# Another replay order and other PSUM banks for the same instructions of a Zipformer block on one core

## The chip, the cores and the metric

The kernel runs on one core of a Trainium2 chip. The time is device time in microseconds (us) of one execution. The core's engines each work through a list of instructions of their own: PE (TensorE, matmuls, with a separate queue PEld for loading weights), ACT (ScalarE, activation functions), DVE (VectorE), POOL (GpSimd) and SP (SyncE, which here only issues DMA transfers). Engines wait for one another through semaphores. Lower is better.

## The reference

`x` has 2 batch elements of 4000 tokens of 144 channels in bf16. There are 4 heads of 36 channels; the feed-forward parts are 576 wide; the convolution has 5 taps.

```python
h = _layernorm(x); h = _silu(h @ w_ff1a) @ w_ff1b; x = x + 0.5 * h
q, k, v = heads(_layernorm(x) @ w_qkv)              # 4 heads of 36
p = _softmax((q @ k^T) * 36 ** -0.5)                # 4000 x 4000 for each head
x = x + heads_back(p @ v) @ w_o
h = _layernorm(x) @ w_pw1; a, b = h[..., :144], h[..., 144:]
h = a * _sigmoid(b)
c = sum over 5 taps of hp[:, i:i + T, :] * dw[i]    # depthwise, padded by 2 on each side
x = x + _silu(c) @ w_pw2
h = _layernorm(x); h = _silu(h @ w_ff2a) @ w_ff2b; x = x + 0.5 * h
return _layernorm(x)
```

## The kernel before

**Tiling.** The 8000 tokens are 16 chunks of 500 (CH), 8 for each batch element; a chunk is 4 blocks of 125 rows (TB), kept in SBUF as X. For a chunk, `pre` does the first feed-forward part and q, k, v; then comes attention; `post1` does the output projection with its residual, the next normalisation and the gated pair (GLU); `post2` the convolution, its residual, the second feed-forward part, the last normalisation and the store. The attention of a chunk is a row of steps, each one key tile of 64 keys and two heads: `emit_S` lets PE compute scores into two PSUM banks, `emit_exp` lets ACT take their exponential (128 x 1000, tile PT), and `emit_O` (`o_quads`) lets PE multiply the result with V. For 190 of the tiles DVE does the exponential instead, in four instructions (`dve_tile`). The work of `pre`, `post1` and `post2` of other chunks is laid between these steps.

**Normalisation.** `ln` takes statistics on DVE (tile ST), variance plus epsilon (RS), a power of -1/2 on POOL, and then the normalised rows (XN). At the start and at the end this is DVE's work but for the power, two blocks at a time; in between POOL does all but the statistics. The rows are then transposed for the matmuls (tile XT): on PE at the start and the end, and otherwise by `blocks`: a 32 x 32 transpose on DVE, a write to DRAM by four transfers ("rows"), and a read back by two, both from SP's queue. SP's queue also holds the loads of X and the stores of the output.

**The order.** All instructions are recorded through one method, `Rec.op` (so that nearly every row of the profile has the same line, L419, the one that issues them), while a planner with costs of its own walks the threads. The recorded instructions form blocks: those that one step of the planner gave to one engine. `Rec.reorder` then replays them in an order that is written out in the table ORDER. It has a string for each engine with one character for each block; the character's place in ALPHABET less 45 is by how many places the block goes later or earlier than in the planner's list (`P` is no shift; `~` starts a larger one):

```python
codes, shift = [ALPHABET.index(c) for c in table[e]], []
...
    shift.append(c - 45)
...
    at[i + shift[i]] = blk
lines[e] = [o for blk in at for o in blk]
```

Semaphore waits are derived afterwards (`Rec.finish`), from what each instruction reads and writes. An engine works strictly in its list's order, so a block that waits holds up all behind it. The table PLACES has a digit for each of the 1724 PSUM tiles, the first bank that it gets (`Rec.place`); a tile waits for those who used its banks before.

**The start.** The load of chunk 0 comes in two halves by SP (`X[0:TB, 0:2, :]` and `X[0:TB, 2:NB, :]`, semaphores of their own). DVE's list starts with memsets (`zero_k`, `early`, `setup_v`) and the statistics of chunk 0's blocks 0, 1 and 2, 3. PE runs filler matmuls on the identity (`warm`) until there is something to do.

Of the kernel before, what the change touches and what calls it, by code (L numbers as in the profile page):

```python
# [13 lines left out]
H = 4  # L14
# [25 lines left out]
        "PPPPPPPPQOPPPPROQNPPQRPQLPPRPTPUPNIZOVOKVVL~OOKOK~OUHINSNLMMMOPNOJSOOL[I[KMYMKOGRNJHFKOOOE^NNN_dMKLM"  # L40
        "nXMJ@LJMFMYGaJNKMJhLLLLljKKKKKKWKMMWNKK`BJJJQRecHFSIGKH]QKMRGKPMJJMMQTNPNXTRSUJUJJJSLPMPPQUQQNKOTOOR"
        "OQLPPPPPYOOPN[NNNOMfRNLYULMIMOS^KIMOJNaNNQMNHPPaUOMQNYKPSPPQUSVV^QQ^_Q5<@QCPMKIMNNTQMSMNSNUOYQKMMOQQ"
        "^MSOORNOPPCOORPZP^O]OOO[OCNOQEHMUJNNTOMR[MQWXMPMMNNDMPXSNNZMMTMMMTMPLMPP]OOOOQQNUKNOMQMP]WNOMPNVKYPN"
        "JNQHNOOPQQQMPPQOPUP]MNNNOOTNNOMNWOPPMPNOW]VNN[MMHMKYMMQ]YKI`JLQYJJKV[KHMJTLJOJPMQORPVMQNYMN]MN[bLLLL"
        "LMNLPRPKWOYFMNOVNOHXXMKOLNNNN[[_MMMTLLTKKKLJOOPRP`MO_OMNOMPQLLMRMMMPPPQOSYP[MOOISOLNPPIPSPTOLRNNWPNO"
        "QQMMPUQRN[QQQRJFPPPPJQQSPPKQQNPPPPVPPQOPVXOOPNDNPRROSVSYNFWMPYUPNDPJFPNPTOPYOLOPNQ[NLNRPMRLNNOPhUNZM"
        "MMNLNNPMMWYLPNZKNLMF[LPPSLVINLNOMWQNYPYPLQHKOSNORPGPPPS[OOLOOPPYLNNNVOMNOM^QMNTOO_KMMNOMPPLPNQOYL]RY"
        "LMKLMMPLY]KLNNQXMRXSLI[MDObNOENPMMNSNNQMMWNNNOSVNiKZNNQOTFNNOMXXUMMMM?TLLIYMQXXLLMMQZMJJ`ORLMUMKQYNL"
        "INPMMUVNLNOMYPMOORNNRUNKPNO_ROQLSSKMQMKPROLPSOORNOSOOOTVNNNNSNTMTMNNOVXNOMORLSNVXIMSYLMKLN^XYNLMNHMM"
        "WLLMXMNYMOLNNXMNXMMVMM[SLJLLZN^OLNNJUbLLLQNLPRGNNOOOPNRNOPPPeOOOOPSOOORROf`OPNO^@QDLJLMOLTKLTMTRKGMQ"  # L50
        "QNUOPNROYYPZOHNbILLLLbTLLSLLLLPLM_M[MMMMMcMMMMNLMOdZMNNNNIMMMMXMNNVOMKMMZNOUaMMMQMM]^HOMKNNNJZMKM[LM"
        "QgLLLMWMMMMU]LLLV^MQJMWTMHBHMZSKL[PLLZTMK_bMMIGbMPLPQMSVCKRKSMBINPPSPVOLOOOOZQNNS[MMMMNSMOMNO]aNNcMM"
        "MMMMMMNLNNNZWNZMZPNKPMYBENOPJYNNPMPQOLQNPPRRO[YQJNOPQOPXFPHPNOOOPWOOOOOOXPMTQOLOK^OXNNOMPPPLPPHQQNgR"
        "cOLQOMPNOOOOdRM@LdOJOIPIOOOJOOOOJOOPNUPNOOQQYLQ]NLZ[LLLdWKIKLLLWULE]LLLLLOMWRcKLLLNZM[PMMRILNKZJ`[JK"
        "MOLLUbKeJLLYKOUKMMMMMY=KMNNZNL^NLNNNNNN_NNNOQQNPTHNN_NLOOO^QMNPKO^QQM_JFPLOPJMNPPLPhMPROOPQOWOWNNNNU"
        "U?NO[HMTOOOCNOOOQO[OQOUOOOPHVORPYMGNPPMOVNN[QOVKPNZPGLOY]OPLOPPPBHOOORPRROR`OPWQNZCLNNPQZKMQETOJOMNU"
        "OOOOOPPPP[OOPNQNQRLMVZLOTNKPLLOOPPVPNOVOMRMOSLOOPPPPPZOWOMNNN]NLMPRTLNZUNLQMNYWNRAOPTOSHRNDQOPTOOPNP"
        "UOUQ_LROQQIQFNOYPNUKQNKTNKOQRSTNQNRXFQOQVQULMVEMPPP[PPPQODZcMPMMQINPKMPNOOOPRMNPPPQOZOOOOOQOMOOPXOOZ"
        "NNNNNN`NPWMXNNOPNKOCNOXPNOQOMZQMUOKXMZP[^XIMMOOKPABPJOPPPXOOQOPPPRIOPSOVSMOTKQUKLPNQNPXQOMROMPMQWQMU"
        "OQNJMQQNPQQTQOKTNO[NQOPQOUOOVRMUZPNVSYMN`OQK6TNNZ;NLNVMMMMTMMVWMMdMNLMNOO]N[MMM]XLJKKRK^aJHNPPRKNX>N"  # L60
        "OJLOMNPPPSPPQTVOOQVPLPQOAPQOPQOQZVOLOMRUMKL[MPMOOQWMMNNYOLNORNNNOYVNNNOWLMMROORROH]QNQMNOXNOMPMUPKMY"
        "NTOLORSTJMWOPPFObTYLNQSMKG_MKMNN`RMKLOLR]MKPNgIMMMNOYNKNNNNNZTMQXILIXJLMQLYOSJMNPU_]JLOKRSMMHLMOMQOW"
        "OOQOMOUNPNUQRM`YYLOREKNKKV[LJNLOSQJN`KPXLObLMWNK]MIJQLLOUO^LDLTKQNLVLQ^MMQRMSFMUWMNNWMG^MTRMJYLRPNGO"
        "TYMN[aXVMWQHKLJMFRf[M5LMNSNNKNLZMNNQRPLJTOIOO`^YMMNLMMOMKMMNRSLROLPPTOVOOLVNNPMOO_ROOLRNNNQQMMRNNPQO"
        "VQNNTVNLMPMZUO_QOLLOSNNVNOQNNQSPSWNWNPNVNN[QMNRPNQVXMNPMXPPXKUNNNNVQM~N?ZRMMMPXRLM]LLSMNLNQOMO[NQORO"
        "TNPPY[K]SBNNKILMNNPNPP_TNNOMN_NNNNNPMMSNNNNQYMPNOVZNNYJLN`]MMRMNRCOPLPNVOQ@USLMMNQOQ[NOOUNNNNNNTNQNN"
        "[QNNOOZRMMPMZPNPGM`N`NLMMR[OPLQNGGLOZWNOOOFPMMOPPPPQOQOQRRRSQJRPYPVPQOPPU@QUXEPMRIQNQJQQUPQUPIPYJNPW"
        "WPKOKVOYHJiMPPLJOPTOOIOPROOIUOMNORLQLQQQMRPQQLTOQRRSUUOHHNRMO"
    ),
    "act": (  # L70
        "PPPPPPPPPPPPPRTNNOOPPQOPPPPPPXPNOSNNNNPPPPQOPPSPNOQZQORKRSLLOQQJPPPPQQNQOPPPPPPPPPQQQMPPQOPPPPPPPPRO"
        "OPQOPQQNPPPPPPPPPPPPPPPPPPPPPPPPPPPPPPPPPPPPPPPPPPPPPPPPPPPPPPPPPPPPPQOPPPROSNOOPPPPPPPPPQOPPPPPPPPP"
        "QOPPPPPPPPPPPQOPPPPPPPPPPPPQOPPPPPPPPPPPRPNPQOPPPPPRPNPPPPPPPPPPPPPPPPPPPPPPPPPPPPPPPPPPPPPPPPPPQOQQ"
        "NPPPPPPPPPPPPPPPPPPPPPPPPPPPPPPPPPPPPPPPPPPPPPPPPPPPPPPPPPPPPPPPPPPPPQOPPPPPPPPPPPPPPQOPPQOPPPPPPPPP"
        "PQOPPPPPPPPPPPPPPPPPPPPPPPPPPPROOPQOPPPPPPPPPPPPPPPPPPPQOPPPPQOPPPPPPPPPPPPPPPPPROOQQQMPPPPPPPPPPPPP"
        "PPPPPQOPPQOPPPPPPPQOPPPPPPPPPPQOPPQOPPPPQQQQQKQQNPPPPPPQOPPPPPPPPPPPPPPPQOPPPQOPPPPPPPPPPPPPPPPPPPPQ"
        "OPPPPPPPTOOOOROOPPPPPPPPPPPPPPPQOPQOPPPPPPPPPPQOPPQOPPPPPPPQOPPPPPPPPPPQOPPPPQOQOPPPPPPPPQOPPPPPPPPP"
        "QOPRPNQOPPPPPPPQOPPPPPPPPPPPPPPPPPPPPPQRNOPPPQOPPPPPPPQQNPPPPPPPPQOPPPPPPPQOQOPPQOPPPPPPPPPPQOPPPPPP"
        "PPPQOQOPPPPPPPPPPPPPPPPPPPPPPPPPQOPQQNPPPPPPPPPPPPPPPPPPPPROOPPPPPPPPPPPQQNPPPPPPPPQOPPPPPPPPPPPPPPP"
        "PPPPPQOPPPPPPPRPNQOPPPPPPPQOPPPPPPPPPPPPQOPPPPPPPPPPPPPPPPPPPPPPPPPPPPPPQOPPPPPPPPPPPPPPQOPPPPPPPPPP"  # L80
        "PPPPPPPPPPPPPPPPPPPPPPPPPPPPPQOPPRORPMSPPULOSNRMMPPPPQTPSOKSQOKROORPQQLPPPPPPRORRRWRJRRMHMROO"
    ),
    "dve": (
        "PUO[VM~P6~P6~P)~P6ILIKKLDKMJQRJJJKIKQKKLJKMKOLJWOILJHLJNQNPHFGNNNJMMMMBMWOIKIMINLMNOODNDPSPLORCFVSWC"
        "JDJSIOMBREEMKNCMMMMFNNJMMMMMMNLOPSPROLPPRPNPQOQOQQQMQOQQNPQQNQOPPQOPPQOPPPQOROOPROQVQOYPNOPROSPXURVQ"
        "UU;JNIQQSSSOSQRSSZRSSSKRVQUJ=OO)PROQNPRPRSLPRPQJQOPPPUOPNPQ`VPVOVOMEULFNKNRMRPQQQQIQOPQOQOSOORNTNOPN"
        "QOPQOPPQOQOPPPRPNPROQRMQRPQRPTPPPRPVVPNPSOLQQQQQQ5PPVPPPPPQRHQQQLPPPPPPPPQOPPPPPPPPPROSNPNPPPQSQSLSO"
        "RJQQLQQQQQQQQHPPROSPPTRPNQGQOPQOUQOPLQNRPNPQORUNNOOQNSOOTRUOMTOOPFPQOPPPPPPQQRRRKMRPNPQOPPPPPPPPPPQR"
        "PRPQQQHQOPWOPSOSKTLVOSNUNQMDOPPROOSOPNSQO^PjOOOSNNNCMNTMPLMNTNNNNNOOOPROOROOPRPQQRPJPRSNNQNPQOQOPQOQ"
        "OYRNNNYNOMNSOLRMULQNNOTPPMOQOQOPQOPPPSOPNSOSNPQLPPPPPPPVOOOOOXNOOROQNKUOOOOQNQOPPTTPNLNPPPPPPPPPPQSP"  # L90
        "PLQOPPP]OOOOOOOOOOOOQOQOPQOQOROOPQOWOPNOOOORPNPSPNSSPRSJTJWMRSLLRLMPTRNNQQLQOPPPPPPPPPQQSMPNPRPSPPQJ"
        "PPPPPQQNPQOQQNQOROOPQOPPPRPNPPPQQNPPPPTOOOOPQOPRPNQOQQRSOKQNQOSOOQNQRNOPQOSQRMMPPPPPROQNQOPPPPPQOPPP"
        "PQRPQRRORPQFPPPPPPPPPWPNPNOOOUPNOPNQSNSNNSNORNUQMPMOPROOROVNOOOPQMPPPPPPXQNQMQUNQNSOUQQUCOJOOPPQQNQO"
        "PPUPNOOOPPQRPQQRJQTPLOOTOOOOPPPQVNOQTMQNSQTNTFNNQNQOPPQQNPQOPPPQOQORPSPLOTOOOORORNQSMSNTRPRJRPIROQNQ"
        "OPTQNNTNOOSNSNNOUOOOOOPPPPPPROOROOQOQUROQSUSTGOHKPPPPPQOPQOQOPPQOPPROOQOPPPPPPPPPQRPUPPSORTRPRSUURXS"
        "=KQAQRNQQEPPPPPPPQOQOSOSOhTPMPRMSEOOKOPPPPPPROGNOPPPQRNRNOPQQQMPPPPPQQNQQNQQQQQKQQQRVOXOHOOLOOQNRPNP"
        "PPPPPPPSOOWNSNNQMUQKSOOQJQUN^PhLNKOPPKOKNNNPPMOOOOOOOOQQQRRKNPRPRPSQOQTPTODNRNQNQQUPLPROTRPWMXSNPSQW"
        "RZQUFOSDO7KOPPPTOOSOTOPPIPPPQOPPPPPPTPQMQMPQOPQQNQQRRORRRUQRPUWTQNRSCTRPRRRRDQQRPSPRSQR[RTQNPREO~NKO"
        "RNaNOOOPQMNQYNOPNPTQFNJPRRNNPPPPQOPQOPUPPPPSQOVVFNNNNNPPROOPPPPPROQNPPQQNPPRORPUPTQINLPPQOQOPPPPQOQQ"
        "RMTPPROUQRPFLQRNOPPROOUOXNNNUMNVWL[PRVIGPIOINQNPQQRTUSOITJPKOPSQS`PQQRHRSSTVSWWGRGW<FHMWWMVLLMTMKLO"  # L100
    ),
    "pool": (
        "PPPPPPPROOPPPSOPNPQQQQQQJPPPPPP_PPPPPJOOPQ[NKTMMOMNOSNUMNSNRNTKVNVMPLMPMROQTMOOTVMNNNOQTMOOQXMOOOTNN"
        "OMPPQOPPUOQNNOPPQOPQQNROO"
    ),
    "sp": (
        "PPQOPPPPQOPPPPPPPPPPPPPPWPWMNNNOPLPPPPPPQOPPPPPQRNOPPPPPQOPPQOPPPPPPPPPPPPPPPPPPPPPPPTOPNYNOWNNNNNNN"
        "VOWNNNNPMOPVOZNOMNNOOSNNNPPZOPNOOOOOOOPXOOOOOPPQLPPPPPPQO"
    ),
}  # L110
PLACES = (
    "3054320451505435202310543130213550204405323242301405230054110122532155431241204124012410314032034023"
    "4203421340243310402430043213420342040324304023420342034203420342034203420342034203420342024042045012"
# [2033 lines left out]
```

## Time and profile before

| | |
|---|---|
| median of 3 runs | 875.68 us (875.66 to 875.73) |
| profiled execution, its own time | 875.47 us |
| its span (first to last instruction) | 873.7 us |
| mean granted TensorE clock | 0.996 |
| busy, share of the span | PE 97%, ACT 97%, DVE 94%, POOL 34% |
| transfers | 28.82 MB, mean 33 GB/s |
| exps on ACT, 128 x 1000, from 46 to 840 us | 794 of them, busy 735.8 us |

Rows of the timeline read: start, length, engine, line, operation, output tile `<-` input tiles, partitions x elements and type, how many in a row (x), and in brackets the idle time of the engine just before and what ended it. A row of several instructions has the time from the first one's start to the last one's end. SPq and ACTq rows are issues of transfers. Rows of waits give the engine and its output tile, who was waited for, the sum in us, how often, and the longest. Tables of stretches give start and end of each, its length, the busy time and instructions of each engine, the granted clock of PE, the share of the DMA engines' time, and GB/s.

### The profile page before, as it was taken

Reading aid. Unit: us, or ns where it says so; the run is one execution under the profiler, and the core shown is the slowest. Engines: PE = TensorE matmul, PEld = TensorE weight load, DVE = VectorE, ACT = ScalarE, POOL = GpSimd, SP = SyncE. Lnnn points to the kernel's source line nnn. Section 1 sums busy time; section 2 is a strip of 40 time slices with the busy share of each in tenths; the row PEclk is TensorE's granted clock in tenths of the full one; section 3 lists DMA queues with packets and bytes.
Section 4 is the critical chain, followed back from the end, with each engine's and each line's share of the span. In section 5 each row is a group of like instructions: output and inputs, shape, how many; then the busy total and the mean of one; then the engine's idle time right before and its main releaser. Section 6 shows DMA issues by size and latency. Waiting matters only on the chain.

```text
span 873.7 us, 27060 instructions
## 1 busy us (share of the span) xinstructions
PE 844.9 (97%) x11419; PEld 385.8 (44%) x11419; DVE 825.3 (94%) x1821; ACT 845.2 (97%) x1098; POOL 294.8 (34%) x573
## 2 busy tenths in 40 slices
PE   8999999999999999999999999999999999999996
PEld 6543444334444434443444444445434433444466
DVE  8978999999999999999989999899999999999987
ACT  6799999999999999999999999999999999999985
POOL 6650450341325141152211552621414413022433
PEclk9999999999999999999999999999999999999999
DMA  4221101121121020212001120110111011001111
GB/s 100 51 57 32 24 17 43 35 66 31 27 53 39 16 51 11 44 22 48 21 4 29 24 56 17 31 29 16 38 31 25 20 31 21 18 15 37 25 29 35
DMA packets 114353, 28.82 MB, mean 33 GB/s; under 512 B 101090, under 2 KB 114230, under 8 KB 114230
## 3 DMA queue, kind: packets, MB, share of 16 engines
q1 hardware_dynamic: 112646, 26.39, 13.9%
q8 instruction: 90, 1.47, 0.7%
q10 hardware_dynamic: 1584, 0.69, 0.3%
q14 instruction: 33, 0.27, 0.1%
HBM read 13.44 MB, written 13.61 MB: 31 GB/s over the span
## 4 chain that ended last, share of the span: by engine, by line
ACT 65%; PE 20%; DVE 11%; POOL 3%; issue 1%; POOLq 0%; ACTq 0%
ACT PT L419 60%; PE PS L419 20%; ACT TH L419 5%; DVE PT L419 4%; DVE ST L419 2%; DVE XN L419 2%; POOL XN L419 1%; DVE X L419 1%; POOL RS L419 1%; DVE HT L419 1%; DVE RS L419 0%; DVE AN L419 0%; DVE U L419 0%; DVE KT L419 0%; DVE XT L419 0%
## 5 line engine op out<-in xcount | busy, mean ns | idle before, releaser
L419 ACT ACTIVATE PT<-PS 128x1000 bf16<-128x1000 f32 (+1 forms) x818 | 751.6, 1050 | 3.4 <-PE PS L419 2.8
L419 PE MATMUL PS<-QT,KT 64*64 64x500 bf16 x3968 | 419.4, 384 | 12.2 <-ACT PT L419 7.4
L419 PE MATMUL PS<-PT,VA 64*37 64x500 bf16 x4728 | 406.5, 372 | 1.8 <-DVE QT L419 1.0
L419 DVE TENSOR_SCALAR PT<-PS 128x500 int16<-128x500 f32 x380 | 250.7, 670 | 7.5 <-PE PS L419 5.7
L419 PEld LDWEIGHTS PS<-QT,KT 64*64 64x64 bf16 x3968 | 124.6, 104 | 230.4 <-ACT PT L419 130.3
L419 POOL TENSOR_SCALAR RS<-ST 125x4 f32<-125x4 f32 x130 | 38.3, 295 | 473.8 <-DVE ST L419 467.2
L419 PEld LDWEIGHTS PS<-PT,VA 64*37 64x37 bf16 x4728 | 142.4, 96 | 94.9 <-issue 14.1
L419 DVE TENSOR_SCALAR PT<-PT 128x1000 uint16<-128x1000 uint16 x380 | 154.7, 421 | 2.3 <-PE PS L419 1.0
L419 POOL TENSOR_SCALAR XN<-X,RS 125x144 bf16<-125x144 bf16 x260 | 144.9, 587 | 9.6 <-DMA out_dram<-XN 1.5
L419 DVE TENSOR_TENSOR PT<-PT 128x1000 bf16<-128x1000 bf16 x190 | 127.6, 675 | 0.8
L419 ACT ACTIVATE TH<-PS 128x500 bf16<-128x500 f32 (+3 forms) x194 | 102.3, 550 | 5.2 <-PE PS L419 5.2
L419 POOL TENSOR_TENSOR RS<-RS,NHALF 125x4 f32<-125x4 f32 (+2 forms) x93 | 93.9, 1013 | 33.6 <-DVE RS L419 28.1
L419 DVE SCALAR_TENSOR_TENSOR HT<-TH,PS 128x500 bf16<-128x500 bf16 (+1 forms) x135 | 81.2, 614 | 8.4 <-ACT TH L419 7.8
L419 PE MATMUL PS<-XT,WA 128*128 128x500 bf16 (+4 forms) x288 | 75.6, 368 | 3.4 <-DVE PT L419 0.8
L419 DVE BATCH_NORM_STATS2 ST<-X 125x6 f32<-125x288 bf16 x160 | 65.8, 447 | 1.6 <-DMA X<-in_x_dram 1.2
L419 DVE SCALAR_TENSOR_TENSOR X<-PS,X 125x288 bf16<-125x288 f32 x128 | 56.7, 450 | 4.9 <-PE PS L419 3.6
L419 PE MATMUL PS<-WB,HT 128*125 128x144 bf16 (+1 forms) x640 | 52.8, 230 | 0.6 <-ACT HT L419 0.2
L419 PEld LDWEIGHTS PS<-WB,HT 128*125 128x125 bf16 (+1 forms) x640 | 44.4, 136 | 13.9 <-issue 4.3
L419 PEld LDWEIGHTS PS<-XT,WA 128*128 128x128 bf16 (+1 forms) x288 | 21.4, 98 | 36.4 <-issue 10.3
L419 POOL COPY U<-U 128x2 bf16<-128x2 bf16 (+1 forms) x54 | 12.2, 266 | 56.2 <-DVE U L419 56.2
L419 DVE STREAM_TRANSPOSE XN<-XN 128x320 f32<-128x320 f32 x54 | 27.0, 501 | 4.0 <-POOL XN L419 4.0
L419 PE MATMUL PS<-U,DG 128*128 128x250 bf16 (+6 forms) x204 | 27.8, 263 | 0.1
(95 smaller groups left out, 521.0 us busy)
## 6 DMA issues: line engine op xcount, KB each, us to landing
rows<-XN SPq DMA_DIRECT2D x216, 40.0 KB, 2.0
XT<-rows SPq DMA_DIRECT2D x56, 128.0 KB, 2.0
rows<-AN SPq DMA_DIRECT2D x60, 40.0 KB, 2.0
X<-in_x_dram SPq DMA_DIRECT2D x15, 140.6 KB
XTQ<-rows SPq DMA_DIRECT2D x26, 70.3 KB
out_dram<-XN SPq DMA_DIRECT2D x13, 140.6 KB
XT<-rows SPq DMA_DIRECT2D x56, 16.0 KB, 1.9
out_dram<-XN SPq DMA_DIRECT2D x3, 70.3 KB
```

The lines of the kernel that those rows point to most:

```text
L419: ins = getattr(eng, o.name)(*o.a, **o.k)
```

## The change

Only the two tables ORDER and PLACES change: the strings of all five engines, and 174 of the 1724 digits. The recorded instructions, their operands and the planner stay as they are. The new order comes from a re-timing in which loads of X and stores in SP's queue hold up the transfers behind them.

Counted in blocks that follow another block than before: PE 1953 of 2855, DVE 949 of 1689, ACT 133 of 1093, POOL 80 of 125, SP 64 of 157. Most shifts are one to three places, the largest on PE 30 and on DVE 36. Decoded, with the before's start times as names for blocks:

- DVE, start. Before: `zero_k` memsets, memsets of XN, statistics of chunk 0's blocks 0 and 1 (3.81), two memsets of `setup_v` (4.25), RS of blocks 0 and 1 (4.51), a memset, statistics of blocks 2 and 3 (4.86), their RS (5.30), XN of blocks 0 and 1 (5.45), a memset, XN of blocks 2 and 3. After: a memset, `zero_k`, two memsets, statistics of blocks 2 and 3, two memsets of `setup_v`, statistics of blocks 0 and 1, RS of blocks 2 and 3, a memset, RS of blocks 0 and 1, XN of blocks 0 and 1, XN of blocks 2 and 3, a memset.
- The first blocks of PE, ACT and POOL keep their order; the first power on POOL and the first transposes on PE are those of blocks 0 and 1.
- SP: stores change places with transposing transfers. Chunk 0's (484.90) goes ahead of the XT read at 460.70, chunk 5's (632.67) ahead of that at 618.83, chunk 6's (671.15) ahead of that at 623.65, chunk 10's (828.60) ahead of the write at 789.04, chunk 9's (794.33) behind the write at 838.41.
- POOL: the normalisations before those stores move with them; halo copies of the convolution come later (that of chunk 9 from 586 to 630); between 541 and 562, the normalisation before chunk 4's store goes ahead of that in chunk 5's second feed-forward part, and chunk 6's ahead of that before chunk 3's store.
- ACT: some 25 exchanges of an exp with a neighbouring activation in the middle, 35 of 54 blocks in the last part.
- DVE, tail: chunk 15's first residual of the output projection (846.53) goes six places earlier, residuals of chunks 13 and 11 go later.

```diff
 ORDER = {
     "pe": (
-        "PPPPPPPPQOPPPPROQNPPQRPQLPPRPTPUPNIZOVOKVVL~OOKOK~OUHINSNLMMMOPNOJSOOL[I[KMYMKOGRNJHFKOOOE^NNN_dMKLM"
+        "PPPPPPPPQOPPPQRNQNPPQSPPLPPRPUQOQOI[OPPMUVM~OOLNL~OUIKNTNLMMMOPKPLSOOL[H[KLYMKOHRNLHFKOOOC[NNNb_MKLM"
...
     "act": (
-        "PPPPPPPPPPPPPRTNNOOPPQOPPPPPPXPNOSNNNNPPPPQOPPSPNOQZQORKRSLLOQQJPPPPQQNQOPPPPPPPPPQQQMPPQOPPPPPPPPRO"
+        "PPPPPPPPPPPPPRTNNOOPPQOPPPPPPXPNOSNOMNPPPQQNPRROMPPZQOSLRSMKOQQIPPPPQQNQOPPPPPPPPPQQQMPPQOPPPPPPPPQO"
...
     "dve": (
-        "PUO[VM~P6~P6~P)~P6ILIKKLDKMJQRJJJKIKQKKLJKMKOLJWOILJHLJNQNPHFGNNNJMMMMBMWOIKIMINLMNOODNDPSPLORCFVSWC"
+        "QWPPXK~P7~P;~P,~P*LIMJLLELNKRPIJJKMHQKKLJKMKOLJVMIMKHLJQQMPIFFMNNKMMMMAMXOIKIMIOLLMOODODPSOLNQCEVSWC"
...
     "pool": (
-        "PPPPPPPROOPPPSOPNPQQQQQQJPPPPPP_PPPPPJOOPQ[NKTMMOMNOSNUMNSNRNTKVNVMPLMPMROQTMOOTVMNNNOQTMOOQXMOOOTNN"
-        "OMPPQOPPUOQNNOPPQOPQQNROO"
+        "PPPPPPPQOPPPPSOOOPPPPPPPTOOOOPP[OOOOOPNOOO^NSWMMMMNNYMTLMXLSLLZSKOJQXJMNSMMRMMPRRSMMOPPSOOSNPNPPRTNP"
+        "PLPPPROOTOPNOROOPPPPPQRNO"
     ),
     "sp": (
-        "PPQOPPPPQOPPPPPPPPPPPPPPWPWMNNNOPLPPPPPPQOPPPPPQRNOPPPPPQOPPQOPPPPPPPPPPPPPPPPPPPPPPPTOPNYNOWNNNNNNN"
-        "VOWNNNNPMOPVOZNOMNNOOSNNNPPZOPNOOOOOOOPXOOOOOPPQLPPPPPPQO"
+        "PPQOPPPPQOPPPPPPPPPPPPPQWPXLNNNQQLQKPPPPPPPPPPPPROOPPPPPQOPPROOQOPPPPPROOPPPPPQOQOPPPQOQOTOOVNNOOOOP"
+        "UOXNNNNPNOOROSNOOPPPPXOOOOOZNQMMOOOOOOQOXOOOOOOORNOPPPQQN"
...
 PLACES = (
-    "3054320451505435202310543130213550204405323242301405230054110122532155431241204124012410314032034023"
+    "0152305245314031252310543130213550204405323242310405230054110122532155431241204124012410314032034023"
...
```

## The prediction before the result

> **What bounds the kernel now.** I read the page first, then busy time by stage, the waits, and then the first 12 us instruction by instruction, because there the orders differ in a way that a single row can price. The page, and busy time in four stages (columns: stretch, its length, busy us and instructions of PE, PE's weight loads, DVE, ACT, POOL, then the granted clock, DMA share, GB/s):
>
> ```profile
> span 873.7 us, 27060 instructions
> PE 844.9 (97%) x11419; PEld 385.8 (44%) x11419; DVE 825.3 (94%) x1821; ACT 845.2 (97%) x1098; POOL 294.8 (34%) x573
> ACT 65%; PE 20%; DVE 11%; POOL 3%; issue 1%; POOLq 0%; ACTq 0%
> ...
> 0.00:46.00 46.00, 41.55 (x440) 27.62 (x441) 40.53 (x126) 33.70 (x64) 31.67 (x72) 0.96 0.32 73
> 46.00:840.00 794.00, 776.48 (x10673) 335.20 (x10670) 756.62 (x1595) 790.29 (x979) 251.00 (x481) 1.00 0.14 31
> 840.00:870.00 30.00, 26.91 (x312) 23.00 (x310) 28.15 (x102) 20.39 (x54) 12.17 (x20) 0.99 0.12 31
> ```
>
> ACT bounds the middle: 790.29 of 794 us, and most of the chain that ended last (third line) is ACT's too. The front, 0 to 46, leaves ACT 12.3 us idle; the tail is DVE's (28.15 of 30). The waits of ACT in the middle, and those of the whole run that a transfer of X, of the rows or of the output ended (us in total, times, longest):
>
> ```profile
> ACT PT L419 <- PE PS L419: 2.0, 7, 0.4
> ACT TH L419 <- PE PS L419: 0.8, 2, 0.6
> ...
> POOL XN L419 <- DMA out_dram<-XN: 1.5, 1, 1.5
> PEld PS L419 <- DMA XT<-rows: 1.4, 4, 0.5
> DVE ST L419 <- DMA X<-in_x_dram: 1.2, 1, 1.2
> ```
>
> ACT waits for PE alone. What the re-timing corrects, transfers held up by X loads and stores, ends 4.1 us of waits in all, and 1.2 of these are the first load of the run.
>
> **The change part by part.** No instruction is added or removed, so no busy time is. What can change is idle time, priced stage by stage.
>
> *1. The start.* DVE now takes the second half of chunk 0 first. Rows of the first 12 us:
>
> ```profile
> 1.52 5.01 PE L419 MATMUL PS<-IDENT 128*128 128x128 bf16 x50 [1.52 <-POOL NHALF L419]
> 3.81 0.46 DVE L419 BATCH_NORM_STATS2 ST<-X 125x6 f32<-125x288 bf16 x1 [1.21 <-DMA X<-in_x_dram]
> 4.25 0.20 DVE L419 MEMSET WPZ<- 128x176 uint32 x1
> 4.51 0.10 DVE L419 TENSOR_SCALAR RS<-ST 125x2 f32<-125x2 f32 x1
> 4.62 0.33 DVE L419 MEMSET XN<- 128x320 uint32 x1
> 4.70 1.55 POOL L419 TENSOR_TENSOR RS<-RS,NHALF 125x2 f32<-125x2 f32 x2 [0.35 <-DVE RS L419]
> 4.86 0.40 DVE L419 BATCH_NORM_STATS2 ST<-X 125x6 f32<-125x288 bf16 x1
> 5.45 0.69 DVE L419 TENSOR_SCALAR XN<-X,ST,RS 125x144 bf16<-125x144 bf16 x2
> 6.37 0.39 PE L419 MATMUL PS<-IDENT,XN 125*128 125x125 bf16 x4
> 10.40 0.46 DVE L419 SCALAR_TENSOR_TENSOR X<-PS,X 125x288 bf16<-125x288 f32 x1 [0.20 <-PE PS L419]
> ```
>
> Before: statistics of blocks 0 and 1 at 3.81, as soon as the first half of X is there; their variance (RS) at 4.51, the power on POOL at 4.70, XN at 5.45, transposes on PE at 6.37. After, DVE's order is: statistics of blocks 2 and 3 (the 4.86 row), two memsets (4.25 to 4.51), statistics of blocks 0 and 1, RS of 2 and 3, a memset, RS of 0 and 1. The orders of POOL, PE and ACT there are the old ones: the first power, the first transposes are still those of blocks 0 and 1. So all of them wait until the second half of X has landed. When that is, the packets of SP's queue tell (packets, MB, share; from 0 to 3.3, to 3.8, to 4.2 us):
>
> ```profile
> q1 hardware_dynamic: 126, 0.07, 9.2%
> ...
> q1 hardware_dynamic: 225, 0.13, 12.6%
> ...
> q1 hardware_dynamic: 260, 0.14, 12.7%
> ```
>
> Each half is 0.07 MB. The first had moved by 3.3 and released DVE at 3.81, 0.5 later. The second had not at 3.8 and had at 4.2; it had landed by 4.86, where DVE found it without waiting. With the same 0.5 it lands near 4.6 (ends 4.2 and 4.86). RS of blocks 0 and 1 then follows after statistics (0.44 to the next start), memsets (0.26), statistics (0.44), RS of 2 and 3 (0.11) and a memset (4.62 to 4.86, 0.24): 4.6 + 1.49 = 6.09 instead of 4.51, 1.58 late (1.18 to 1.84). Before, XN ended at 6.14 and its transposes ran at 6.37, behind PE's filler matmuls: about 0.1 of slack. PE, POOL and ACT have nothing else, so the chain to the residual at 10.40 moves by **+1.5** (bounds +1.1 and +1.7).
>
> *2. What the front takes back.* DVE's idle time in the rest of the front, and the granted clock of its one slow stretch:
>
> ```profile
> 10.40:20.00 9.60, 8.03 (x112) 5.85 (x110) 9.38 (x33) 7.49 (x18) 7.19 (x13) 1.00 0.50 118
> 20.00:30.00 10.00, 8.88 (x74) 3.53 (x75) 8.51 (x21) 8.06 (x13) 8.23 (x18) 0.83 0.26 49
> 30.00:46.00 16.00, 15.76 (x165) 10.02 (x164) 15.96 (x43) 13.11 (x25) 10.23 (x20) 1.00 0.21 43
> ...
> 12.68:16.09 3.41, 2.63 (x33) 1.00 0.52 132
> 19.50:22.92 3.42, 2.12 (x19) 1.00 0.07 12
> 22.92:26.33 3.41, 3.29 (x18) 0.50 0.25 43
> ```
>
> DVE is idle for 0.22 + 1.49 + 0.04 = 1.75 us between 10.4 and 46. All of it used would swallow the delay; most lies in the slow stretch, where PE is the bound and gives nothing. I take **-0.4** (ends 0 and -1.5).
>
> *3. The clock.* The second fence (PE busy, clock) has PE at half clock from 22.92 to 26.33, right after a stretch of the same length in which PE was busy for 2.12 of 3.42; a stretch with 2.63 of 3.41 kept full clock. After the change PE idles about 1.5 us between 6.4 and 8, so the stretch 5.85 to 9.26, one of the same raster and so far without a gap in the rows around 6.37, holds about 1.9 of 3.41, under the 2.12 that was followed by half clock; the next 3.41 us would then run at half. It costs at most 3.41/2 = 1.7, at least 0; PE there also runs fillers that may stretch freely, so I take **+0.6**. [...]
>
> *4. The middle.* Of PE's 2855 blocks 1953 get another predecessor, of ACT's 1093 only 133. The idle rows understate ACT's waiting, since an exp overlaps the next by some 0.16 us:
>
> ```profile
> 110.19 4.72 ACT L419 ACTIVATE PT<-PS 128x1000 bf16<-128x1000 f32 x5
> ...
> 177.62 1.90 ACT L419 ACTIVATE PT<-PS 128x1000 bf16<-128x1000 f32 x2 [0.41 <-PE PS L419]
> ...
> 563.17 0.59 ACT L419 ACTIVATE TH<-PS 128x500 bf16<-128x500 f32 x1 [0.56 <-PE PS L419]
> ...
> 681.95 13.47 ACT L419 ACTIVATE PT<-PS 128x1000 bf16<-128x1000 f32 x15
> 731.68 0.84 ACT L419 ACTIVATE TH<-PS 128x500 bf16<-128x500 f32 x1
> ...
> 731.57 0.41 PE L419 MATMUL PS<-QT,KT 64*64 64x500 bf16 x4
> ```
>
> Fifteen exps from 681.95 start every (13.47 - 1.06)/14 = 0.886; five from 110.19 every 0.915, late scores and no idle time shown. So I compared, for each ACT instruction, its slot and that of the matmuls it reads in both orders, by before's start times. The late inputs that come earlier (177.62 the largest, its PE block three places up; also 563.17) are worth 4.7 us at most. Against that, some 30 groups of exps get their scores later than their slot, by 0.1 to 0.5: at 731.68 an exp now stands where the TH stood, but its scores end at 731.57 + 0.41 = 731.98, 0.3 late. Together about 8.5 if each counted in full. They don't: a delayed ACT finds its next late input in time. The ends are -4.7 and +8.5; I take a quarter of the net 3.8, **+1.0**, because the place of an exp that was delayed before absorbs a new delay.
>
> *5. Stores and transposing transfers.* SP's queue around a store (start, issue time):
>
> ```profile
> 549.41 2.56 SPq L419 DMA_DIRECT2D rows<-XN  x4
> 553.38 0.82 SPq L419 DMA_DIRECT2D XT<-rows  x2
> ...
> 567.10 3.32 SPq L419 DMA_DIRECT2D rows<-AN  x4
> 571.83 0.82 SPq L419 DMA_DIRECT2D XT<-rows  x2
> ```
>
> From write to read-back takes 3.97 undisturbed and 4.73 behind a store. The moves exchange one hold-up for another: Chunk 0's store (c0) stands ahead of the XT read at 460.70, c5's and c6's ahead of those at 618.83 and 623.65 (their LNs pass LN c8 on POOL, which has room), and c9's behind the write at 838.41, ahead of the last XT read. On POOL LN c6 gets ahead of the LN of c3's store, and that of c4's store ahead of LN c5. Each is worth up to 0.8 for one transfer that ACT doesn't wait for; the 1.4 us that PE waits for XT is the whole prize, 0.8 late at 842 the price: **0**. [...]
>
> *6. The tail.* Same work, c15's first residual six DVE places ahead of c13's and c11's. DVE idles 30 - 28.15 = 1.85; all of it is the gain, c9's store the loss of 0.8. DVE is full from 846, so: **0**.
>
> Sum: 875.47 (873.7 of it span) + 1.5 - 0.4 + 0.6 + 1.0 = 878.2; the median shown is 0.21 above the profiled execution: **878.4**.
>
> **Rivals.** *The front swallows its delay*: DVE's 1.5 of idle time is used, no dip comes, the middle's items cancel: 875.7 to 877.2. For it: ACT has 12.3 us of idle time there. Against: from 30 to 46 DVE has 0.04.
> *Faster*: the middle recovers its late scores. Place: the PE blocks behind ACT's late inputs, 177.62 and 563.17 first; price -4.7; it decides once the recovery exceeds the front's 1.7 by 1.75, that is from 3.5: 875.68 + 1.7 - 4.7 = 872.7 at best, about 873.5. Against it: the 8.5 of new lateness.
> [...]
> *Much slower*: new lateness counts for half or more, 4 to 5, as PE has just 17.5 us of slack in 794: 881 to 882.
> *The order doesn't matter at all*, because before's queues were never held up: that leaves the front alone, which is the forecast less 1, 877.4, and lies within its range.
>
> **How the numbers follow.** No change means within 0.2%, 1.75 us: 873.93 to 877.43, about what a measurement can tell. Forecast, 876.9 to 879: 0.33, of which 0.05 lies below 877.43. Clock halved in full, 879 to 880.2: 0.20. Front swallowed: 0.17. Faster: 0.14, of which 0.02 is within the bound. Much slower: 0.16. Faster 0.12, same 0.02 + 0.05 + 0.17 = 0.24, slower 0.64. The range leaves out the faster case and the end of the much slower: 875.0 to 881.8. The likeliest case's own range is 876.9 to 879.
>
> **What would show it.** Step 1: DVE's first statistics wait to about 4.6, RS of blocks 0 and 1 near 6.1, first transposes near 7.9, residual near 11.9; wrong if the second half lands by 4.2. Step 2: ACT's busy time from 0 to 46 about 1.5 lower. Step 3: a clock of 0.5 in 9.3 to 12.7. Step 4: ACT's idle time from 46 to 840 within 3 to 6 us, and no idle at 563 or 177. Step 6: DVE busy about 28 in its last 30 us. What would make it wrong: scores late in runs of exps, without one idle row to show it.

## The result and the profile after

The changed kernel takes 878.46 us (median of 7 runs, 877.95 to 878.67) where the kernel before took 875.66 (7 runs, 875.00 to 875.79): a ratio of 1.0033, with a 95% interval of 1.0023 to 1.0043. It is 2.8 us slower, and 878.4 was forecast; but three of the forecast's terms were wrong and made up for each other, as the experiments show.

From the page of the changed kernel's profiled execution, the span, the engines' busy time and the shares of the chain that ended last:

```profile
span 876.9 us, 27061 instructions
PE 844.1 (96%) x11419; PEld 384.2 (44%) x11419; DVE 825.7 (94%) x1821; ACT 845.0 (96%) x1098; POOL 292.9 (33%) x573
ACT 54%; PE 25%; DVE 14%; POOL 4%; issue 1%; DMA 1%; SPq 0%; POOLq 0%; ACTq 0%
```

Its busy time in the same four stages as before (the last one longer, since the span is), PE, PEld, DVE, ACT and POOL, then the granted clock, DMA's share and GB/s:

```profile
0.00:46.00 46.00, 39.46 (x423) 26.13 (x423) 39.27 (x122) 32.33 (x63) 30.53 (x70) 1.00 0.31 72
46.00:840.00 794.00, 777.16 (x10683) 334.77 (x10682) 757.46 (x1597) 790.23 (x979) 250.26 (x484) 1.00 0.14 31
840.00:870.00 30.00, 27.53 (x318) 23.35 (x315) 27.35 (x95) 21.57 (x56) 10.89 (x19) 1.00 0.10 26
870.00:877.00 7.00, 0.00 (x0) 0.00 (x0) 1.59 (x8) 0.90 (x2) 1.24 (x2) 0.68 0.17 48
```

No engine has more work: ACT's busy time is 845.0 against 845.2. The middle is as full as it was, 790.23 of 794 us on ACT against 790.29. What is missing is at the ends. In the front ACT does 32.33 us of work by 46 us where it did 33.70, 1.37 less. In the tail DVE has 27.35 of 30 where it had 28.15, and 1.59 us of its work lie behind 870, where there was none. ACT's waits from 46 to 840 us:

```profile
ACT PT L419 <- PE PS L419: 2.0, 7, 0.4
ACT XTQ L419 <- PE PS L419: 0.4, 1, 0.4
ACT TH L419 <- PE PS L419: 0.2, 1, 0.2
```

They are 2.6 us, 0.5 less than the 3.1 of the kernel before. Since both kernels have the same instructions, each exp can be found in both traces. Late against the same exp in the kernel before, in us (columns: the kernel before's time of the exp; the last column is the end of the last instruction on DVE):

| profiled execution | 19 | 59 | 199 | 275 | 551 | 592 | 820 | end of DVE |
|---|---|---|---|---|---|---|---|---|
| changed | 1.41 | 1.06 | 0.38 | 1.12 | 1.61 | 1.01 | 0.82 | 2.06 |

So the start loses 1.4 and gives 0.35 of it back by 59 us; the middle wanders within 1.2 us and ends 0.24 better than it began; the tail loses 1.24 on DVE, and another 1.1 behind DVE's end, for the spans differ by 3.2. The rows of the start that answer those of the prediction:

```profile
4.48 0.46 DVE L419 BATCH_NORM_STATS2 ST<-X 125x6 f32<-125x288 bf16 x1 [1.53 <-DMA X<-in_x_dram]
...
5.18 0.40 DVE L419 BATCH_NORM_STATS2 ST<-X 125x6 f32<-125x288 bf16 x1
...
5.90 0.10 DVE L419 TENSOR_SCALAR RS<-ST 125x2 f32<-125x2 f32 x1
...
7.58 0.39 PE L419 MATMUL PS<-IDENT,XN 125*128 125x125 bf16 x4 [1.21 <-DVE XN L419]
...
11.63 0.46 DVE L419 SCALAR_TENSOR_TENSOR X<-PS,X 125x288 bf16<-125x288 f32 x1
```

DVE waits for X until 4.48 instead of 3.81, takes the statistics of blocks 2 and 3 first, and has RS of blocks 0 and 1 at 5.90 instead of 4.51. PE, which had its filler matmuls up to the first transposes, now waits 1.21 us for XN, and the first residual follows at 11.63 instead of 10.40.

### The profile page after: what moved, and what is told of

Read it like the earlier page. It is cut to its first block, busy times and chain, and to the rows that moved or that the text cites. A ratio compares the mean times of both kernels' runs of the same rounds, so it can differ in the third digit from the quotient of the medians.

```text
span 876.9 us, 27061 instructions
## 1 busy us (share of the span) xinstructions
PE 844.1 (96%) x11419; PEld 384.2 (44%) x11419; DVE 825.7 (94%) x1821; ACT 845.0 (96%) x1098; POOL 292.9 (33%) x573
## 4 chain that ended last, share of the span: by engine, by line
ACT 54%; PE 25%; DVE 14%; POOL 4%; issue 1%; DMA 1%; SPq 0%; POOLq 0%; ACTq 0%
ACT PT L419 49%; PE PS L419 25%; DVE PT L419 6%; ACT TH L419 4%; POOL RS L419 2%; DVE ST L419 2%; DVE XN L419 2%; POOL XN L419 2%; DVE X L419 1%; DVE HT L419 1%; DVE KT L419 1%; DVE QT L419 0%; DVE AN L419 0%; DMA XT<-rows 0%; DVE VA L419 0%
## 5 line engine op out<-in xcount | busy, mean ns | idle before, releaser
L419 POOL TENSOR_TENSOR RS<-RS,NHALF 125x4 f32<-125x4 f32 (+1 forms) x93 | 91.4, 987 | 38.5 <-DVE RS L419 33.1
L419 PE MATMUL PS<-XT,WA 80*128 80x500 bf16 (+5 forms) x288 | 74.9, 364 | 2.9 <-DMA XT<-rows 0.9
L419 PE MATMUL PS<-U,DG 128*128 128x250 bf16 (+7 forms) x204 | 28.4, 264 | 0.1
L419 PE MATMUL PS<-IDF,QT 128*125 128x128 f32 x128 | 23.0, 302 | 0.4 <-DVE QT L419 0.4
## 6 DMA issues: line engine op xcount, KB each, us to landing
X<-in_x_dram SPq DMA_DIRECT2D x15, 140.6 KB
out_dram<-XN SPq DMA_DIRECT2D x13, 140.6 KB
```

The lines of the kernel that those rows point to most:

```text
L419: ins = getattr(eng, o.name)(*o.a, **o.k)
```

## The experiments

Each was timed beside the kernel before on the same chip; differences are those of the medians. An order or a bank table that changes from one kernel's to the other's does so, on each engine, at a place where both have done the same blocks.

**The start alone, undone and done.** The changed kernel with the first 14 places of DVE's order as before, and the kernel before with these as changed:

```diff
 # the changed kernel, start of ORDER["dve"]
-"QWPPXK~P7~P;~P,~P*LIMJLLELNKRPIJ...
+"PUO[VM~P7~P;~P,~P*ILIKKLDKNJRPIJ...
 # the kernel before, start of ORDER["dve"]
-"PUO[VM~P6~P6~P)~P6ILIKKLDKMJQRJJ...
+"QWPPXK~P6~P6~P)~P6LIMJLLELMKQRJJ...
```

> The changed kernel with the first 14 places of DVE's order as before (statistics of blocks 0 and 1 first); all else as changed. In the traces the exps of the changed kernel run 1.05 to 1.15 us late from 60 us on. Theory (the start's delay passes through the whole middle to the end, since ACT has no idle time to take it back): first residual back at 10.4, exps from 60 us on about 1.1 us earlier, 877.3 us. Rival (a late start is taken back later, since PE and DVE have slack in the middle, and the middle's own lateness sets the end): 878.2 to 878.5 us.

> The kernel before with the first 14 places of DVE's order as changed (statistics of blocks 2 and 3 first). Theory (additive): first residual near 11.6, 876.7 us. Rival (the front swallows the delay in DVE's and ACT's idle time): 875.7 us. [...]

Undone, it took 877.12 us, 1.73 above the kernel before (ratio 1.0016, 1.0007 to 1.0025), so the start carries 1.1 of the 2.8. Done alone, it took 876.43, 1.04 above (1.0010, 1.0001 to 1.0019). In the first trace the residual is back near its old time, in the second it is where the changed kernel has it:

```profile
10.49 0.44 DVE L419 SCALAR_TENSOR_TENSOR X<-PS,X 125x288 bf16<-125x288 f32 x1
```

```profile
5.90 0.10 DVE L419 TENSOR_SCALAR RS<-ST 125x2 f32<-125x2 f32 x1
...
11.63 0.46 DVE L419 SCALAR_TENSOR_TENSOR X<-PS,X 125x288 bf16<-125x288 f32 x1
```

With the start alone the exps are 1.24 late at 19 us, 0.92 at 59 and 1.01 at 820: what the front hasn't taken back by 59 us goes through 760 us of a full ACT (790.25 of 794 us from 46 to 840) unchanged.

**Why the start is late.** The changed kernel with the two halves of chunk 0's load issued in the other order:

```diff
-op("sp", "dma_start", X[0:TB, 0:2, :], ... q="x0", ...)
 op("sp", "dma_start", X[0:TB, 2:NB, :], ... q="x0b", ...)
+op("sp", "dma_start", X[0:TB, 0:2, :], ... q="x0", ...)
```

> The changed kernel with the two halves of chunk 0's load issued in the other order, blocks 2 and 3 first, as DVE takes them. Theory (the start's delay of RS of blocks 0 and 1, 1.39 us, is half a wait for the second half of X, 0.67 later on DVE, and half the instructions put ahead of it): RS near 5.25, first residual near 11.0, exps 0.6 us earlier than the changed kernel's, 877.8 us. Rival (the wait is all): 877.1 us. Rival (the wait does not matter, other loads set the start): 878.4 us.

It took 877.33 us, 1.80 above the kernel before (1.0022, 1.0013 to 1.0031), 1.0 better than the changed kernel's 2.80. RS of blocks 0 and 1 and the residual, 0.6 us earlier than in the changed kernel:

```profile
5.29 0.10 DVE L419 TENSOR_SCALAR RS<-ST 125x2 f32<-125x2 f32 x1
...
11.03 0.46 DVE L419 SCALAR_TENSOR_TENSOR X<-PS,X 125x288 bf16<-125x288 f32 x1 [0.17 <-PE PS L419]
```

That is the half that was put down to the wait for the second half of X; the instructions put ahead of RS keep the rest (5.29 against 4.51). The time gained 1.0, which is nearer the rival's figure than the theory's. But in this one trace the last store is also 0.7 us shorter than in the changed kernel's (it varies, see below), so the rows of the start, and not the time, tell the two apart.

**The tail, undone and done.** Order and banks from about 815 us on (SP's list from 765, the last place there where both have done the same):

```diff
 # blocks of pe, act, dve, pool, sp
-changed order throughout
+changed order for the first 2695, 1007, 1560, 103, 138; from there the order before
 # and the reverse
-order before throughout
+order before for the first 2695, 1007, 1560, 103, 138; from there the changed order
```

> The changed kernel with the order and banks of before for everything from about 815 us on (SP from 765). The exps of the changed kernel are 0.8 late at 820 and its span ends 3.2 late, so the tail carries 2.4. Theory (the tail's order itself costs 2.0 to 2.4, by chunk 11's residual and normalisation, moved to the end of DVE's list): 876.2 us. Rival (the tail is long because what comes late from the middle, its transfers and stores, comes late): 877.8 to 878.5 us.

> The kernel before with the changed order and banks from about 815 us on (SP from 765). Theory (the tail's order itself): 877.8 us. Rival (lateness from the middle): 875.7 to 876.2 us.

Undone: 876.82 us, 1.43 above the kernel before (1.0015, 1.0006 to 1.0024), so the tail carries 1.4. Done alone: 878.38, 2.99 above (1.0030, 1.0019 to 1.0042). The two don't agree because the seam, the place where one order gives way to the other, costs something itself: the exps lose 0.6 and 0.8 us right at 815 us in the two kernels, where neither parent does. With that taken off, the tail carries 1.4 + 0.6 = 2.0 and 3.0 - 0.8 = 2.2. A seam behind the last exp has no such jump in the exps:

```diff
-changed order throughout
+changed order for the first 2780, 1034, 1604, 108, 138; from there the order before
```

> The changed kernel with the order and banks of before only for what follows the last exps (from about 838 us; SP from 765). It splits the tail: 815 to 838 stays as changed. Theory (all of the tail's loss arises behind the last exp: DVE idle 1.2 us more in 838 to 846, and 1.1 us at the last store): 876.1 to 876.6 us. Rival (half of it arises at 815 to 838, in the order of the last exps): 877.3 us or more.

876.70 us, 1.11 above (1.0012, 1.0004 to 1.0021): undone, what follows the last exp gives back 1.7 of the 2.8. This seam costs something too, on DVE: the exps are 0.56 late at 820 us, but the first reciprocal behind the last exp (RD, the division that ends an attention result) is 1.21 late, since DVE waits for PE there for 1.5 us instead of 0.8; all of DVE's rows behind it are 1.2 late to the end. So the tail carries 1.7 + 0.65 = 2.3, as near as single traces tell.

**Where in the tail.** Two things stand out there. One is the last store. ACT's last XN in the kernel before, and in the changed one (a row of two instructions that end 0.90 later):

```profile
869.94 0.90 ACT L419 ACTIVATE XN<-X,RS 125x144 bf16<-125x144 bf16 x2 [1.71 <-DVE RS L419]
```

```profile
871.99 0.90 ACT L419 ACTIVATE XN<-X,RS 125x144 bf16<-125x144 bf16 x2 [3.20 <-DVE RS L419]
```

From its end to the end of the span it is 873.7 - 870.84 = 2.9 us before, and 876.9 - 872.89 = 4.0 after. The changed kernel's transfers from 870 to 877 us hold what the other hasn't there, chunk 11's whole output, issued at 870.94, 2.0 us ahead of the last store:

```profile
out_dram<-XN SPq DMA_DIRECT2D x1, 140.6 KB
```

The 4.0 is one of the longest of its kind: in the traces of the five kernels with this tail that last part takes 4.0, 4.0, 3.7, 3.3 and 3.2 us, and in those of the nine without chunk 11's store there 2.75 to 2.95. So the store costs 0.3 to 1.2 us, 0.8 in the mean. Chunk 11's second feed-forward part had been moved by up to 14 us on DVE, its normalisation to right ahead of chunk 15's last RS. So this was put back alone (g0 are the first two blocks of a chunk):

```diff
 # the changed kernel; chunk 11 only
-dve: residual g0 at 1671, statistics 1677, RS 1681, XN 1685 (ahead of chunk 15's last RS)
+dve: behind its other half (1658), chunk 12's XN (1663), chunk 13's RS (1665) and XN (1672)
-pe: matmuls of g0 at 2840, bank 1; sp: store behind chunk 15's first; pool: power at 122
+pe: behind its other half (2830), bank 0; sp: store ahead of chunk 15's; pool: behind 118
```

> The changed kernel with one thing put back in the tail: the last matmuls, residual, normalisation and store of chunk 11 come ahead of chunk 15's, as before (the matmuls of its first half use bank 0). In the changed kernel DVE ends 1.2 us later than the lateness at 825 us explains, with chunk 11's XN (1.00 us) right ahead of chunk 15's last RS, and its 140.6 KB store is issued 2.0 us ahead of the last one, which then takes 4.0 us from its XN to the end instead of 2.9. Theory (both come from chunk 11's place): DVE ends 1.0 to 1.2 earlier and the last store lands 1.1 faster, 876.2 us. Rival (DVE is full there, so work moved ahead only pushes chunk 15 back): only the store's 1.1, 877.4 us. Rival (other shifts of the tail): 878.4 us.

877.94 us, 2.41 above the kernel before (1.0028, 1.0017 to 1.0038): only 0.4 of the 2.8 came back. The trace has both sides of it:

```profile
872.55 0.90 ACT L419 ACTIVATE XN<-X,RS 125x144 bf16<-125x144 bf16 x2 [2.16 <-DVE RS L419]
```

From its end to the end of the span (876.2) it is 2.75 us: the last store is as quick again as before, and 1.25 us came back there. But DVE ended 0.5 later than in the changed kernel, not 1.0 earlier. The blocks that were moved ahead of chunk 15's pushed it back, and where chunk 11's statistics had filled a wait for POOL's power, DVE now stood idle:

```profile
869.29 0.16 DVE L419 SCALAR_TENSOR_TENSOR RS<-ST,RS 126x2 f32<-126x2 f32 x1 [0.81 <-POOL RS L419]
```

So the theory held for the store and fell for DVE: this way of putting chunk 11 back doesn't return DVE's 1.2 us. Where these arise can still be read. Chunk 15's last statistics and the RS behind them, in the kernel before and in the changed one, where chunk 11's XN stands between:

```profile
868.26 0.46 DVE L419 BATCH_NORM_STATS2 ST<-X 125x6 f32<-125x288 bf16 x1
868.75 0.17 DVE L419 TENSOR_SCALAR RS<-ST 125x2 f32<-125x2 f32 x1
```

```profile
869.23 0.46 DVE L419 BATCH_NORM_STATS2 ST<-X 125x6 f32<-125x288 bf16 x1
869.91 1.00 DVE L419 TENSOR_SCALAR XN<-X,ST,RS 125x144 bf16<-125x144 bf16 x4 [0.22 <-POOL RS L419]
870.82 0.16 DVE L419 TENSOR_SCALAR RS<-ST 125x2 f32<-125x2 f32 x1
```

The statistics are 0.97 late, little more than the exps at 820 us (0.82), and RS is 2.07 late: 1.1 of DVE's 1.24 us arise here. In the four other kernels with this tail the step is 1.1 as well.

The other thing that stood out is DVE's idle time right behind the last exps. Busy time from 838 to 846 us in the kernel before, then in the changed one (columns as above: PE, PEld, DVE, ACT, POOL), with the waits of DVE in this stretch:

```profile
838.00:846.00 8.00, 7.88 (x74) 5.80 (x75) 6.92 (x18) 6.29 (x16) 0.78 (x2) 1.00 0.20 42
```

```profile
838.00:846.00 8.00, 7.42 (x80) 5.38 (x77) 5.74 (x14) 6.72 (x17) 0.73 (x1) 1.00 0.26 60
```

```profile
DVE HT L419 <- ACT TH L419: 1.8, 2, 1.1
```

6.92 against 5.74: 1.18 us more idle time on DVE, which was taken for the 1.24 that DVE ends later. That reading doesn't hold. The kernel before has an idle time of its own just ahead of the stretch, a wait of 1.67 us for POOL that ends at 837.88 and that the changed kernel hasn't; from 825 us on, DVE is busy for as long in both (first the kernel before):

```profile
825.00:846.00 21.00, 17.76 (x42) 1.00 0.21 47
```

```profile
825.00:846.00 21.00, 17.83 (x41) 1.00 0.18 39
```

And with the order of before from 838 us on, DVE is busy for only 5.56 us from 838 to 846, though that kernel is the quicker one. The experiment that was built on the reading: part of the wait for TH arises because a TH now stands behind ACT's table switch (the load of another activation table, 1.28 us). The two were exchanged:

```diff
 # the changed kernel, ORDER["act"], blocks 1035 and 1036
-table switch; TH of tile m1
+TH of tile m1; table switch
```

> The changed kernel with two neighbours on ACT exchanged: the second TH of chunk 14's feed-forward part (tile m1) ahead of the table switch of 1.28 us at 838.39, as before, instead of behind it. In the changed kernel DVE waits 0.73 us for it at 840.39 and has 1.2 us more idle time in 838 to 846 than before. Theory (that idle time is this wait, and DVE sets the tail): DVE's HT of m1 near 839.0, 0.5 to 0.8 us faster, 877.8 us. Rival (ACT or PE set that stretch, DVE only waits elsewhere): 878.3 to 878.5 us.

878.05 us, 2.46 above the kernel before (1.0026, 1.0016 to 1.0037), 0.34 better. The HT that had waited 0.73 us comes 0.9 earlier, and DVE then waits elsewhere:

```profile
839.48 0.67 DVE L419 SCALAR_TENSOR_TENSOR HT<-TH,PS 128x500 bf16<-128x500 bf16 x1
840.68 0.21 DVE L419 RECIPROCAL RD<-PS 125x8 f32<-125x8 f32 x1 [0.53 <-PE PS L419]
...
841.77 0.21 DVE L419 RECIPROCAL RD<-PS 125x8 f32<-125x8 f32 x1 [0.39 <-PE PS L419]
```

In 838 to 846 DVE is busy for 5.83 us, 0.09 more. So this was the rival: the stretch isn't held by that one wait. The 0.34 is what this trace has elsewhere, exps 0.12 earlier at 820 us and a last store 0.2 shorter, and the step of 1.1 us at chunk 15's last RS is still there. That the order behind the last exps costs DVE this much is shown by undoing it as a whole; which other order would spare it is open.

**The lists of SP and POOL alone.** The kernel before, with these two as changed from 60 to 800 us:

```diff
 # the kernel before
-sp blocks 14 to 138, pool blocks 18 to 102: order before
+sp blocks 14 to 138, pool blocks 18 to 102: changed order
```

> The kernel before with the changed order of SP's and POOL's lists alone, from 60 to 800 us: stores, transposing transfers, the normalisations ahead of them and the halo copies; PE, ACT and DVE as before. Theory (ACT doesn't wait for these transfers, a store ahead of one costs 0.8 us of slack): 875.2 to 875.8 us, exps within 0.2 us of before's. Rival (the re-timing's aim is right, held-up transfers set the pace): 874.5 us or less. Rival (the changed lists need the changed order of the others): exps late by 0.5 or more somewhere, 876 us or more.

884.75 us, 9.22 above (1.0108, 1.0095 to 1.0122). The second rival: the lists don't stand alone. The exps lose 4.7 us between 175 and 199 us and 3.5 between 688 and 706. The longest waits of PE in 170 to 215 and of DVE in 685 to 725 us, and SP's queue ahead of the first:

```profile
PE PS L419 <- DMA XT<-rows: 3.7, 1, 3.7
```

```profile
DVE XN L419 <- POOL XN L419: 3.3, 1, 3.3
```

```profile
169.15 2.59 SPq L419 DMA_DIRECT2D rows<-AN  x4
173.16 1.48 SPq L419 DMA_DIRECT2D XT<-rows  x2
174.68 5.19 SPq L419 DMA_DIRECT2D rows<-XN  x8
181.30 2.30 SPq L419 DMA_DIRECT2D XT<-rows  x2
```

and the same in the changed kernel:

```profile
165.10 2.60 SPq L419 DMA_DIRECT2D rows<-AN  x4
169.10 0.82 SPq L419 DMA_DIRECT2D XT<-rows  x2
169.97 6.22 SPq L419 DMA_DIRECT2D rows<-XN  x8
177.63 0.82 SPq L419 DMA_DIRECT2D XT<-rows  x2
```

Behind the first wait comes a stretch of 3.41 us at half clock (184.71 to 188.12, see below). The new list puts a read-back, which starts 4.0 us behind its own write (169.15 to 173.16), ahead of two other writes. In the changed kernel PE and DVE deliver that chunk's AN 4 us earlier, so the queue is through in time; with the old order of the others, the two writes and their read-back come 4 us late, and PE waits 3.7.

**The middle alone.** The changed kernel with both ends as before:

```diff
 # dve
-changed order
+order before up to place 15
 # pe, act, dve, pool, sp
-changed order
+order before from 2780, 1034, 1604, 108, 138 on
```

> The changed kernel with both ends as before: DVE's first 14 places, and all that follows the last exps (from about 838 us; SP from 765). What remains is the change of the middle, 9 to 838 us. Theory (the middle's gains and losses cancel, and start and tail carry the whole difference): 875.1 to 875.7 us. Rival (the middle costs something itself): 876 us or more.

875.91 us, 0.32 above (1.0003, 0.9994 to 1.0012): nothing that can be told from no change, and a figure between the theory's and the rival's. In its trace the exps are 0.33 late at 59 us and 0.10 early at 820, and the first reciprocal behind the last exp is 0.56 late: the middle gains 0.4, and the seam at 838 us takes 0.66. Two kernels took the other way, the kernel before with stretches of the changed middle in which its exps gain:

```diff
 # the kernel before
-order before throughout
+changed order from 165 to 240 us and from 385 to 470 us
 # or
+changed order from 165 to 240 us
```

> The kernel before with the changed order and banks in two stretches only, 165 to 240 and 385 to 470 us, where the exps of the changed kernel gain 0.5 and 0.35 us on before's. Theory (gains and losses of the middle are local and stay to the end, as the start's do): exps 0.5 early from 200 us on and 0.8 early from 470 us on, 874.6 us. Rival (what is gained in one stretch is lost at the next late scores): 875.2 to 875.6 us.

> The kernel before with the changed order and banks in one stretch only, 165 to 240 us, where the exps gained 0.55 us in the changed kernel and again in the kernel with two such stretches (the other stretch lost 0.3 there). Theory (local gains stay to the end): exps 0.5 early from 200 us on, 874.9 us. Rival (the tail takes it back): 875.4 us.

The second took 875.30 us, 0.29 below (0.9997, 0.9988 to 1.0005). The exps gained 0.71 from 156 to 199 us, gave 0.17 back by 235, and kept the other 0.54 to 275 and, but for 0.06, to 820; the start of this execution was 0.4 late. The first took 875.54 us, as much as the kernel before (1.0005, 0.9996 to 1.0014), with 7 runs between 874.85 and 875.70 and 4 between 877.17 and 877.42, a gap of 1.5 us that no other kernel here has and that its one trace doesn't explain. In that trace the first stretch gained 0.5, which stayed, and the second lost 0.3 us instead of gaining. By the times both kernels are nearer the rival's figures (875.2 to 875.6 and 875.4) than the theory's (874.6 and 874.9); by the traces the gain of the first stretch stays, as the theory has it. It is too small to tell in the time, and no version here beats both kernels.

## Why the prediction was right in its sum and wrong in three terms

*The start* (+1.5 forecast, and -0.4 that the front takes back, so +1.1): right. DVE waited for the second half of X to 4.48 (4.6 forecast), RS came 1.39 late (1.58), the residual 1.23 (1.5), and the front took back 0.35. Together 1.04 and 1.1 were measured by doing and undoing it.

*The clock* (+0.6): wrong. The step said that PE's idle time would fill one stretch of a raster (a row of equal stretches) of 3.41 us with too little work, and that the next would then run at half clock. There is no half clock in the front of the changed kernel: the granted clock is 1.00 from 0 to 46 us. The raster lies elsewhere in each of the traces compared here. In the kernel before the record of the granted clock begins at 5.85 us, and the clock changes at 22.92, 26.33 and 869.42, that is after 5, 1 and 247 stretches of 3.413 us ((869.42 - 26.33)/247 = 3.4133). In the changed kernel the record begins at 5.50, and the clock falls once, at 872.48, behind the last matmul, after 254 of them ((872.48 - 5.50)/254 = 3.4133). First the changed kernel, then the middle alone (clock falling at 871.70) and the lists of SP and POOL alone, each on its own raster:

```profile
5.50:8.91 3.41, 2.11 (x32) 1.00 0.38 113
8.91:12.33 3.42, 3.23 (x36) 1.00 0.46 134
```

```profile
11.54:14.95 3.41, 1.88 (x30) 1.00 0.60 156
14.95:18.36 3.41, 3.41 (x38) 1.00 0.35 86
```

```profile
181.29:184.71 3.42, 0.00 (x0) 1.00 0.20 50
184.71:188.12 3.41, 3.27 (x24) 0.50 0.41 119
```

A stretch without work was followed by half clock, one with 2.12 us of work in the kernel before too, but one with 2.11 in the changed kernel was not, nor one with 1.88. So from 1.88 to 2.12 us of 3.41, 55 to 62%, PE's busy time in a stretch doesn't tell whether the clock halves; what else decides is open. The mistake was to make a threshold of a single dip and to carry the raster over from one execution to another. No run shows the term, nor the full 1.7 us to which the forecast gave a chance of 0.20: in the five traces with the new start that were read from 6 to 14 us (the changed kernel, the start done alone, the tail undone, chunk 11 put back, the halves exchanged) PE idles there, with 2.70 to 3.12 us of work from 6 to 10, and the granted clock is 1.00.

*The middle* (+1.0): wrong in size, and by the traces in sign. The place at 177.62, where the wait was to vanish, kept half of it:

```profile
178.49 1.90 ACT L419 ACTIVATE PT<-PS 128x1000 bf16<-128x1000 f32 x2 [0.21 <-PE PS L419]
...
551.40 7.29 ACT L419 ACTIVATE PT<-PS 128x1000 bf16<-128x1000 f32 x8 [0.43 <-PE PS L419]
```

The wait of 0.56 at 563 is gone, and one of 0.43 stands at 551. New lateness came (at 275 and 551 us) and was mostly taken back at a later late place (592), as the step argued; at 731.68, the place that it names, the exps go from 1.04 to 1.20 late and are back at 0.94 by 738. From 59 to 820 us the exps of the kernels with the changed middle gain 0.2 to 0.5 us. The middle alone costs 0.32 +- 0.8 us in the time, with a seam that costs 0.66 in its trace; "a quarter of the net" was still too much.

*Stores and transfers* (0): right for the change as a whole, as the middle alone shows, and wrong as a general price. "Up to 0.8 for one transfer" is what the kernel before shows with a store ahead (4.73 against 3.97 us from write to read-back). With the lists of SP and POOL alone a read-back ahead of other writes cost its whole wait, 4.0 us, and PE waited 3.7; in the changed kernel PE's longest wait for such a read is 0.6, and its weight loads' 0.9.

*The tail* (0): the step that failed. It said that the work is the same and DVE is full from 846, so only c9's store could cost. Undone, the tail gives back 1.4 to 1.7 us, and with what the seams cost it carries 2.0 to 2.3. The step overlooked two things that the orders show. The end isn't DVE's last instruction but the last store, and a store of 140.6 KB was put 2 us ahead of it (0.3 to 1.2 us in the traces). And a full DVE doesn't mean that the end stays: the last link of chunk 15's chain now waits behind chunk 11's XN (1.1 us). The first is shown by putting it back. The second is read from the rows of five traces; putting chunk 11 back alone didn't return it.

The clock's 0.6 and the middle's 1.0 and more were too much, the tail's 2.0 to 2.3 too little. That they cancel, and that the sum came out within 0.1 us, is luck; only the start was right by its mechanism.

## What to carry to other kernels

A change of order is priced at its two ends first: what the first chain waits for (here a load that lands second, asked for first), what stands ahead of the last chunk's last instructions, and what is queued ahead of the last store. In between, where one engine is full (here ACT, 790.2 of 794 us), local gains and losses of a few tenths stayed until the next late place and nearly cancelled (0.2 to 0.5 us gained from 59 to 820 us), and they were not worth a term each. Queue lists and engine lists were only good together: SP's and POOL's alone cost 9.2 us.

## What was not expected of the hardware

Kernels with the same order as the kernel before in the first 60 us differ in their fronts. The stretch from 22 to 26 us of the kernel before, and of the kernel with the two stretches (PE busy, clock):

```profile
22.00:26.00 4.00, 3.44 (x24) 0.61 0.27 47
```

```profile
22.00:26.00 4.00, 3.17 (x30) 1.00 0.28 47
```

The exps of the second are 0.24 early at 24 us already, ahead of most of the slow stretch, 0.64 at 30 and 0.35 at 59: the half clock cost 0.4 us, and 0.1 of it is left at 59. Two other kernels with this order and without the half clock, 0.6 and 0.7 late at 24 us, say the same (0.5 and 0.4, with 0.2 and 0.1 left). At 59 us the fronts of these traces lie between 0.35 early and 0.57 late. So a single trace tells a front to about half a us, and the term of a front has to be taken from medians. And a store of 140.6 KB, issued 2 us ahead of the last one on the same queue, made the last part 0.3 to 1.2 us longer (3.2 to 4.0 us against 2.75 to 2.95), by very different amounts in kernels with the same order there. In what way the earlier store does it, no run here shows.
